# Three-bank exponentials in the last half of a four-layer transformer kernel, with the score ring and the probability buffers each made one tile

## The chip, the cores and the metric

One core of one Trainium2 chip. The metric is the device time of one launch in microseconds (us); lower is better. The kernel before takes 2383.65 us in the median of the four runs beside which the changed kernel was timed (2382.35 to 2387.67). Two names recur: PSUM is the memory into which the matmuls of TensorE (PE) write in this kernel, and a *bank* is a piece of it of 512 fp32 columns by 128 partitions, as the code cuts its tiles; SBUF holds the other tiles.

## The reference, cut to what matters

```python
def _A_ref(x, wqkv, w_phi, wo):      # linear attention on softmax features (cut)
    ...
def _B_ref(x, wqkv, wo):             # ordinary attention
    B, S, D = x.shape                # 1, 2048, 1024
    H = 32; Dh = D // H              # 32 heads of 32
    qkv = ...                        # (x @ wqkv) split by heads
    scores = jnp.einsum("bhqd,bhkd->bhqk", q, k) * (Dh ** -0.5)
    p = _softmax(scores, axis=-1)
    o = jnp.einsum("bhqk,bhkd->bhqd", p, v)
    return ... @ wo
def reference(...):                  # four layers: A, B, A, B
    x = A_x
    x = x + _A_ref(_layernorm(x), A_wqkv, A_w_phi, A_wo)
    x = x + _B_ref(_layernorm(x), B_wqkv, B_wo)
    x = x + _A_ref(_layernorm(x), A_wqkv, A_w_phi, A_wo)
    x = x + _B_ref(_layernorm(x), B_wqkv, B_wo)
```

Each B layer needs 32 x 2048 x 2048 exponentials, which is 1024 instructions of 128 x 1024 on ScalarE (ACT). That is the "first" and the "last" attention below; the rest is projections and the linear layers.

## The kernel before

The kernel is emitted by a scheduler in Python: it keeps a model of the engines' clocks, and at each point decides which matmul TensorE issues next. A *step* of attention takes two ring buffers, writes four row-tiled score matmuls (two into each), and starts two exponentials, one for each buffer. That holds for a unit of 512 queries; units of 256 or 128 queries fill the same buffers with more and shorter matmuls. The sums (probabilities times V, and times ones) go to two `work` banks. Whenever no step may start, TensorE does sums, then other projections, then fillers, which are matmuls without use, there for the clock that the trace shows (more of them took it from 0.84 to 1.00 in a stretch of one run below). Projections may borrow ring banks.

```python
e_t = [sb(f"E{i}", [P, 2, C]) for i in range(NE)]          # nine SBUF tiles, C = 512
e_s = Slots(clk, e_t)
...
ring_t = [pps.tile([P, 2, C], F32, tag=f"ring{i}", name=f"ring{i}") for i in range(3)]   # three PSUM tiles of two banks
work_t = [pps.tile([P, C], F32, tag=f"work{i}", name=f"work{i}") for i in range(2)]
...
def exp_chain(u, kks, e, buf):
    E = yield ("take", e_s)
    n = u.n * len(kks)
    yield ("op", "S", c_act(2 * n), lambda x: nc.scalar.activation(
        out=E[:, :, 0:n], in_=ring_t[buf][:, :, 0:n], func=ACT.Exp, scale=INV_SQRT_DH))
    ring.give(buf)
    sums.append((u, kks, e, E))

def emit_step():
    ...                                                    # cut: bookkeeping
    bufs = [ring.take(), ring.take()]
    for i, kk in enumerate(kks):
        c, m = divmod(kk, 2)
        for e in range(2):
            for j in range(2):
                r0 = 64 * (e ^ u.b) + 32 * j
                r = slice(r0, r0 + 32)
                nc.tensor.matmul(ring_t[bufs[e]][:, j, i * n:(i + 1) * n],
                    lhsT=K2[e][c][u.g // 4][r, u.g % 4, m, :], rhs=u.Q[r, e, 0:n],
                    start=True, stop=True, tile_position=(r0, 0), skip_group_check=True)
    for e in range(2):
        clk.start(exp_chain(u, kks, e, bufs[e]), st["t"] + PE_LAT)
```

The code writes no semaphores. The builder puts them in, from which tiles an instruction reads and writes: below, the same slices cut from one ring tile in place of three get other waits, and 2384 us become 3110.

The softmax here doesn't subtract the row's maximum and nothing guards it: scores larger than these inputs give would overflow.

Of the kernel before, what the change touches and what calls it, by code (L numbers as in the profile page):

```python
# [18 lines left out]
P = 128  # L19
D = 1024  # L20
# [197 lines left out]
class Task:  # L218
# [18 lines left out]
    (0, 4, (0,), False, False, (4, 5)), (0, 4, (0,), False, False, (0, 1, 3)), (0, 4, (0,), False, False, (2,)),  # L237
    (0, 4, (0,), False, False, (6, 7)), (4, 4, (0, 1), False, False, (0, 1, 2, 3)),
    (0, 4, (1,), True, False, (0, 1)), (0, 4, (1,), True, False, (2, 3)), (4, 4, (0, 1), False, False, (4, 5)),
    (0, 4, (1,), True, False, (4, 5)), (0, 4, (1,), True, False, (6, 7)), (4, 4, (0, 1), False, False, (6, 7)),  # L240
    (8, 4, (0, 1, 2), False, False, (0, 1, 2)), (8, 4, (0, 1, 2), False, False, (3, 4, 5)),
    (8, 4, (0, 1, 2), False, False, (6, 7)), (0, 4, (2, 3), True, True, (0, 1, 2, 3, 4, 5, 6, 7)),
    (4, 4, (3,), True, False, (0, 1)), (4, 4, (2,), True, True, (0, 1)),
    (4, 4, (2, 3), True, True, (2, 3, 4, 5, 6, 7)), (12, 2, (0, 1, 2, 3), False, True, (0, 1)),
    (8, 4, (3,), True, True, (4, 5, 6, 7)), (8, 4, (3,), True, True, (0, 1, 2, 3)),
    (14, 2, (0, 1, 2, 3), False, True, (2, 3, 4)), (14, 2, (0, 1, 2, 3), False, True, (0, 1)),
    (12, 2, (0, 1, 2, 3), False, True, (2, 3)), (12, 2, (0, 1, 2, 3), False, True, (4, 5)),
    (14, 2, (0, 1, 2, 3), False, True, (5, 6, 7)), (12, 1, (0, 1, 2, 3), False, True, (6, 7)),
# [3 lines left out]
    (0, 4, (0,), False, False, (4, 5)), (0, 4, (0,), False, False, (0, 1, 2, 3)),  # L252
    (0, 4, (0,), False, False, (6, 7)), (0, 4, (1,), True, False, (0, 1, 2, 3)),
    (4, 4, (0,), False, False, (0, 1)), (0, 4, (1,), True, False, (4, 5)),
    (4, 4, (0, 1), False, False, (2, 3, 4, 5, 6, 7)), (4, 4, (1,), True, False, (0, 1)),
    (8, 4, (0, 1, 2), False, False, (0, 1, 2, 3)), (0, 4, (2,), True, False, (0, 1)),
    (8, 4, (0, 1), False, False, (4, 5, 6, 7)), (0, 4, (2,), True, False, (4, 5)),
    (8, 4, (2,), True, False, (4, 5)), (0, 4, (1, 2), True, False, (6, 7)), (0, 4, (2,), True, False, (2, 3)),
    (0, 4, (3,), True, True, (2, 3, 6, 7)), (0, 4, (3,), True, True, (0, 1, 4, 5)),
    (8, 4, (3,), True, True, (4, 5)), (8, 4, (2, 3), True, True, (6, 7)), (4, 4, (2, 3), True, True, (2, 3)),  # L260
    (4, 4, (2, 3), True, True, (4, 6, 7)), (4, 4, (2,), True, False, (0,)), (4, 4, (2, 3), True, True, (1, 5)),
    (4, 4, (3,), True, True, (0,)), (8, 4, (3,), True, True, (0, 1, 2, 3)),
    (12, 4, (0, 1, 2, 3), False, True, (4, 5)), (14, 1, (0, 1, 2, 3), False, True, (2, 3, 6, 7)),
    (13, 1, (0, 1, 2, 3), False, True, (1, 2)), (15, 1, (0, 1, 2, 3), False, True, (0, 1, 2, 3, 6, 7)),
    (12, 1, (0, 1, 2, 3), False, True, (0, 1, 2)), (14, 1, (0, 1, 2, 3), False, True, (0, 1)),
    (12, 1, (0, 1, 2, 3), False, True, (3, 6, 7)), (13, 1, (0, 1, 2, 3), False, True, (0,)),
    (13, 1, (0, 1, 2, 3), False, True, (3, 6, 7)),
# [4 lines left out]
    ('AK', 0, 0, (0,), (0,)), ('AK', 0, 1, (0,), (0,)), ('fold', ('pk', 0)), ('fold', ('pk', 1)),  # L272
    ('AK', 0, 0, (0,), (1,)), ('AK', 0, 2, (0,), (0,)), ('AK', 0, 0, (1,), (0,)), ('AK', 0, 0, (1,), (1,)),
    ('AK', 0, 3, (1,), (1,)), ('AK', 0, 1, (1,), (1,)), ('fold', ('pq', 0)), ('fold', ('pq', 1)), ('DN', 0, 0),
    ('AK', 0, 1, (1,), (0,)), ('AK', 0, 2, (0,), (1,)), ('AK', 0, 2, (1,), (0,)), ('PQ', 0, 0),
    ('AK', 0, 3, (0,), (1,)), ('AK', 0, 1, (0,), (1,)), ('AK', 0, 2, (1,), (1,)), ('AK', 0, 3, (0,), (0,)),
    ('BP', 1, 0, (0,)), ('PQ', 0, 1), ('BP', 1, 0, (1,)), ('AK', 0, 3, (1,), (0,)), ('AO', 0, 0), ('DN', 0, 1),
    ('AO', 0, 2), ('BP', 1, 0, (2,)), ('AO', 0, 1), ('BP', 1, 0, (3,)), ('DN', 0, 2), ('BP', 1, 1, (0, 1)),
    ('BP', 1, 1, (2,)), ('BP', 1, 1, (3,)), ('PQ', 0, 2), ('BO', 1, 0, 1), ('PQ', 0, 3), ('BP', 1, 2, (0,)),
    ('BP', 1, 2, (1, 3)), ('BP', 1, 2, (2,)), ('DN', 0, 3), ('BO', 1, 10, 12), ('BO', 1, 1, 5), ('AO', 0, 3),  # L280
    ('BO', 1, 6, 7), ('BP', 1, 3, (0, 1, 2)), ('AK', 2, 0, (0,), (0,)), ('BO', 1, 7, 10),
    ('AK', 2, 0, (1,), (1,)), ('AK', 2, 0, (0,), (1,)), ('AK', 2, 0, (1,), (0,)), ('BP', 1, 3, (3,)),
    ('PS', 2, 0), ('AK', 2, 2, (0, 1), (0,)), ('PS', 2, 1), ('BO', 1, 5, 6), ('AK', 2, 2, (1,), (1,)),
    ('AK', 2, 1, (0, 1), (1,)), ('PS', 2, 2), ('AK', 2, 1, (0, 1), (0,)), ('BO', 1, 15, 16),
    ('AK', 2, 3, (1,), (0,)), ('DN', 2, 0), ('AK', 2, 3, (0,), (1,)), ('AO', 2, 0), ('AK', 2, 2, (0,), (1,)),
    ('AK', 2, 3, (0,), (0,)), ('BO', 1, 12, 15), ('PS', 2, 3), ('AK', 2, 3, (1,), (1,)), ('AO', 2, 3),
    ('DN', 2, 1), ('BP', 3, 0, (1,)), ('BP', 3, 0, (0,)), ('AO', 2, 2), ('BP', 3, 0, (2, 3)), ('AO', 2, 1),
    ('BP', 3, 1, (0, 1)), ('BP', 3, 1, (2,)), ('BP', 3, 1, (3,)), ('BP', 3, 2, (0, 1)), ('BO', 3, 0, 1),
    ('BO', 3, 4, 5), ('BP', 3, 2, (2, 3)), ('BO', 3, 8, 9), ('DN', 2, 2), ('BO', 3, 5, 7), ('BO', 3, 7, 8),
    ('DN', 2, 3), ('BO', 3, 9, 10), ('BP', 3, 3, (0, 1, 2, 3)), ('BO', 3, 15, 16), ('BO', 3, 2, 3),  # L290
    ('BO', 3, 12, 15), ('BO', 3, 3, 4), ('BO', 3, 10, 12), ('BO', 3, 1, 2),
# [3 lines left out]
class Unit:  # L295
    def __init__(self, l, vi, qt, w, ks, p, part, last):
        self.l, self.vi, self.qt, self.w, self.ks, self.p = l, vi, qt, w, ks, p
        self.q = qt // 4
        self.n = w * P
        self.g, self.b = divmod(p, 2)  # L300
        self.part, self.last = part, last
        kk = [2 * c + m for c in ks for m in range(2)]
        per = 4 // w
        self.steps = [tuple(kk[i:i + per]) for i in range(0, len(kk), per)]
        self.nsum = 0
        self.acc = None
        self.dst = None
        self.nburst = 0
        self.left = 0
        n = len(self.steps)  # L310
        m = -(-n // BURST)
        self.bursts = [2 * ((i + 1) * n // m - i * n // m) for i in range(m)]
        self.Q = None
        self.fast = False


@with_exitstack
def kernel(
# [60 lines left out]
    e_t = [sb(f"E{i}", [P, 2, C]) for i in range(NE)]  # L379
    phibd = e_t[0][:].rearrange("p a (g n) -> p (a g) n", n=P)  # L380
    e_s = Slots(clk, e_t)
# [14 lines left out]
    ring_t = [pps.tile([P, 2, C], F32, tag=f"ring{i}", name=f"ring{i}") for i in range(3)]  # L396
# [175 lines left out]
    def x_chain(l, t, key):  # L572
        yield ("key", key)
        xb = yield from grab(t_x)
# [30 lines left out]
    lo = [0]  # L605

    def slab_next(s):
        lst = slab_use.get(s, [])
        while lst and done_flag[lst[0]]:
            lst.pop(0)  # L610
        return lst[0] if lst else 1 << 30

# [15 lines left out]
    def slab_plan():  # L628
        want = sorted((slab_next(s), s) for s in slab_use)
        for nxt, s in want[:12]:  # L630
            if nxt >= 1 << 30 or nxt > lo[0] + HORIZON:
                break
# [6 lines left out]
            for i, sl in enumerate(slots):  # L639
                if not sl.avail or sl.users or sl.loading:  # L640
                    continue
                if i >= 4 and min((x for x in sl.limits if x > lo[0]), default=1 << 30) <= nxt:
                    continue
                if i in res and res[i] in pinned:
                    continue
                n2 = slab_next(res[i]) if i in res else (1 << 30) + (1 if i < 4 else 2)
# [561 lines left out]
    for l in (1, 3):  # L1208
# [4 lines left out]
        units[-1].fast = units[-2].fast = True  # L1213
    first_unit = {l: min(i for i, u in enumerate(units) if u.l == l) for l in (1, 3)}
# [199 lines left out]
    st = {"log": [], "t": 0.0, "mode": None, "last": -100.0, "ui": 0, "si": 0}  # L1414
# [18 lines left out]
    def step_ready():  # L1433
        if st["ui"] >= len(units):
            return False
        return st["si"] > 0 or unit_ready(units[st["ui"]])
# [9 lines left out]
    def exp_chain(u, kks, e, buf):  # L1446
# [3 lines left out]
            out=E[:, :, 0:n], in_=ring_t[buf][:, :, 0:n], func=ACT.Exp, scale=INV_SQRT_DH))  # L1450
        ring.give(buf)
        sums.append((u, kks, e, E))
# [57 lines left out]
    def emit_sum():  # L1510
# [6 lines left out]
        for i, kk in enumerate(kks):  # L1517
            c, m = divmod(kk, 2)
            end = u.left == 0 and i == len(kks) - 1
            for r0, ld in ((n0, None), (d0, ones)):  # L1520
                for j in range(2):
# [3 lines left out]
                        u.acc[r0 + 32 * j:r0 + 32 * j + 32, 0:n], lhsT=lh, rhs=E[:, j, i * n:(i + 1) * n],  # L1525
# [4 lines left out]
        clk.at(st["t"], lambda E=E: e_s.give(E))  # L1530
# [11 lines left out]
    def get_bank():  # L1542
# [8 lines left out]
        if not halves:  # L1551
# [4 lines left out]
            halves.extend([(b, 0), (b, 1)])  # L1556
# [3 lines left out]
        def rel():  # L1560
            split[b] -= 1
            halves.append((b, i))
            if split[b] == 0:
                halves.remove((b, 0))
                halves.remove((b, 1))
                ring.give(b)
        return ring_t[b][:, i, :], rel
# [38 lines left out]
    while True:  # L1606
# [3 lines left out]
        if ready and len(ring.free) >= 2:  # L1610
# [24 lines left out]
        if clk.heap:  # L1635
# [12 lines left out]
            continue  # L1648
        if left:
# [9 lines left out]
HORIZON = 200  # L1659
T_BULK = 8.0  # L1660
# [39 lines left out]
```

## Time and profile before

Most of the profile of before is in the prediction below; here is the frame for it. A *stretch* runs between the first and the last exponential of an attention.

| stretch of the kernel before | us | ScalarE busy | what sets its length |
|---|---|---|---|
| head (before the first exponential) | 289.4 | 131.5 | TensorE's projections |
| first attention | 1003.1 | 982.3 | ScalarE |
| middle | 126.6 | 58.8 | TensorE |
| last attention, first half | 482.9 | 478.3 | ScalarE |
| last attention, second half | 470.1 | 470.0 | ScalarE |
| tail | 8.3 | 0.0 | output |

Two terms recur. The *granted clock* is the share of full speed at which the trace shows TensorE's clock; a *low-clock window* is one of the stretches of 3.41 us that the trace records at half clock. In the list of waits, each line says who waited for whom, then the us in total, the number of waits and the longest:

```profile
PE ring L1469 <- ACT E L1449: 38.7, 103, 0.8
```

The ring's scores (line 1469) were held up by an exponential 103 times in 1024 steps. Nine times in ten the buffers were free when TensorE came to them.

### The profile page before, as it was taken

The numbers are of one execution on the slowest core, as the hardware profiler recorded it, in microseconds if no ns is written. First come the engines' busy times: TensorE is split into PE (matmuls) and PEld (weight loads), VectorE is DVE, ScalarE is ACT, GpSimd is POOL, SyncE is SP. The second block draws the span as 40 slices with busy tenths as digits, with TensorE's granted clock in tenths as the row PEclk, the third lists the DMA queues.
The fourth block names the chain that finished last, engine by engine and source line by source line (L and its number), as shares of the span: only waits on it lengthen the run. The fifth ranks groups of instructions, "written<-read, shape, count | busy, mean of one in ns | idle before, by whom it ended". The sixth has DMA issues, their size and how long they took to land.

```text
span 2380.4 us, 81956 instructions
## 1 busy us (share of the span) xinstructions
PE 2245.8 (94%) x35942; PEld 1009.7 (42%) x35985; DVE 1321.7 (56%) x2398; ACT 2121.0 (89%) x2501; POOL 400.5 (17%) x502
## 2 busy tenths in 40 slices
PE   6898999999999999998999899999999999999998
PEld 3544544334434333434555453433333333333555
DVE  6885554454545468696567855554533274363223
ACT  5543499999999999999998459999999999999998
POOL 3311101110211112122212210020200031120111
PEclk9999999899999999999999999999999999999999
DMA  6453364364454345354234655554465432230001
GB/s 249 145 157 108 132 193 171 112 199 130 147 141 145 108 133 155 115 142 80 91 101 130 173 135 166 192 140 137 123 198 174 135 125 81 64 110 33 19 22 31
DMA packets 216343, 306.05 MB, mean 129 GB/s; under 512 B 98736, under 2 KB 112560, under 8 KB 213296
## 3 DMA queue, kind: packets, MB, share of 16 engines
q1 hardware_dynamic: 191792, 200.14, 28.9%
q0 software_dynamic: 24192, 100.67, 12.6%
q8 instruction: 281, 4.60, 0.8%
q14 instruction: 78, 0.64, 0.1%
HBM read 195.36 MB, written 86.51 MB: 118 GB/s over the span
## 4 chain that ended last, share of the span: by engine, by line
PE 70%; ACT 16%; issue 7%; DVE 6%; DMA 1%; POOL 0%; SPq 0%; ACTq 0%; DVEq 0%; POOLq 0%
PE work L460 25%; PE work L1524 15%; ACT E L1449 14%; PE ring L1469 14%; PE work L463 7%; PE work L1642 3%; PE ring L463 3%; DVE blk L446 2%; ACT blk L772 1%; DVE sm L814 1%; PE work L1038 1%; DMA xnT<-blk 1%; DMA slab<-in_A_wqkv_dram 0%; DVE kvacc L446 0%; PE work L848 0%
## 5 line engine op out<-in xcount | busy, mean ns | idle before, releaser
L1449 ACT ACTIVATE E<-ring 128x1024 bf16<-128x1024 f32 x2048 | 1901.7, 1211 | 26.6 <-PE ring L1469 23.2
L1524 PE MATMUL work<-E,V 128*32 128x512 bf16 (+2 forms) x5888 | 551.1, 319 | 9.6 <-issue 3.7
L1524 PE MATMUL work<-E,ones 128*32 128x512 bf16 (+2 forms) x5888 | 551.0, 319 | 4.0 <-issue 4.0
L1469 PE MATMUL ring<-Q,K2b 32*128 32x512 bf16 (+2 forms) x2896 | 394.0, 315 | 49.4 <-ACT E L1449 38.1
L446 DVE TENSOR_TENSOR blk<-blk,work 128x512 f32<-128x512 f32 (+1 forms) x301 | 203.7, 680 | 375.5 <-PE work L1524 321.9
L1469 PE MATMUL ring<-Q,K2a 32*128 32x512 bf16 (+2 forms) x2896 | 407.8, 318 | 1.6 <-DMA Q<-qd 0.6
L1524 PEld LDWEIGHTS <-V 128*32 128x32 bf16 x5888 | 243.9, 97 | 158.0 <-issue 70.2
L446 POOL TENSOR_TENSOR blk<-blk,blk 64x512 bf16<-64x512 f32 (+2 forms) x180 | 175.1, 973 | 777.3 <-DVE blk L1314 689.4
L1278 DVE COPY blk<-work 128x512 f32<-128x512 f32 (+2 forms) x184 | 97.1, 528 | 346.4 <-PE work L1524 341.4
L1469 PEld LDWEIGHTS <-K2a 32*128 32x128 bf16 x2944 | 119.3, 91 | 385.1 <-issue 372.9
L1524 PEld LDWEIGHTS <-ones 128*32 128x32 bf16 x5888 | 239.5, 97 | 51.8 <-issue 5.9
L1314 DVE RECIPROCAL blk<-blk 128x128 f32<-128x128 f32 x254 | 229.4, 930 | 2.6
L1642 PE MATMUL work<-ident,ones 128*32 128x512 bf16 x3156 | 222.0, 382 | 2.8 <-DVE blk L446 0.9
L1469 PEld LDWEIGHTS <-K2b 32*128 32x128 bf16 x2944 | 163.3, 91 | 135.5 <-issue 128.7
L460 PE MATMUL work<-slab,blk 128*32 128x512 bf16 x2752 | 179.9, 381 | 0.5 <-DVE blk L1278 0.2
L460 PE MATMUL work<-slab,xnT 128*32 128x512 bf16 (+1 forms) x2560 | 156.5, 367 | 0.9 <-DVE kvacc L446 0.3
L460 PE MATMUL work<-xnT,slab 128*32 128x512 bf16 x2120 | 140.5, 384 | 4.2 <-DMA xnT<-blk 2.5
L463 PEld LDWEIGHTS <-xnT 128*128 128x128 bf16 x818 | 79.1, 99 | 89.9 <-issue 17.2
L460 PEld LDWEIGHTS <-blk 128*32 128x32 bf16 x3404 | 78.4, 96 | 90.5 <-issue 32.9
L463 PE MATMUL work<-slab,xnT 128*128 128x512 bf16 (+1 forms) x485 | 106.7, 373 | 5.5 <-DMA slab<-in_A_wqkv_dram 3.0
L1642 PEld LDWEIGHTS <-ones 128*32 128x32 bf16 x3156 | 71.2, 95 | 89.8 <-issue 40.7
L460 PEld LDWEIGHTS <-slab 128*32 128x32 bf16 x3016 | 70.8, 96 | 86.1 <-issue 35.8
(184 smaller groups left out, 2321.8 us busy)
## 6 DMA issues: line engine op xcount, KB each, us to landing
pd<-blk SPq DMA_DIRECT2D x154, 256.0 KB, 2.5
blk<-pd SPq DMA_DIRECT2D x154, 256.0 KB, 3.4
Q<-qd SPq DMA_DIRECT2D x121, 256.0 KB, 2.8
slab<-in_B_wqkv_dram POOLq DMA_DIRECT2D x30, 1024.0 KB, 6.6
qd<-blk SPq DMA_DIRECT2D x64, 256.0 KB, 2.8
x<-blk SPq DMA_DIRECT2D x48, 256.0 KB, 2.7
blk<-x SPq DMA_DIRECT2D x48, 256.0 KB, 3.8
blk<-in_A_x_dram SPq DMA_DIRECT2D x32, 256.0 KB, 3.9
```

Of the source, the lines that this page charges most:

```text
L446: return ("op", e, cost, lambda x: eng(x).tensor_tensor(out=o, in0=a, in1=b, op=op))
L460: nc.tensor.matmul(o[js], lhsT=l[:, js], rhs=r, start=st, stop=sp, tile_position=(0, 32 * j), skip_group_check=True)
L463: nc.tensor.matmul(o, lhsT=l, rhs=r, start=st, stop=sp, skip_group_check=True)
L772: yield ("op", "S", c_act(C), lambda x, s=s: nc.scalar.activation(out=e[:, s * C:(s + 1) * C], in_=src, func=ACT.Exp, scale=1.0 - 2.0 * s))
L814: yield ("op", "V", c_sb(1024), lambda x: nc.vector.reduce_sum(out=sm[:, 0:32], in_=e3, axis=AX.X))
L1038: nc.tensor.matmul(bank[:, o:o + P], lhsT=e[:, s * C + t * P:s * C + (t + 1) * P], rhs=kvm[:, (2 * gp + gi) * 2 + s, :], start=True, stop= ...
L1278: yield ("op", "V", c_ps(n), lambda e: nc.vector.tensor_copy(out=a, in_=bank[:, 0:n]))
L1314: yield ("op", "V", 0.06 + 0.0063 * P, lambda e, x=x: nc.vector.reciprocal(out=r[:, x:x + P], in_=r[:, x:x + P]))
L1449: yield ("op", "S", c_act(2 * n), lambda x: nc.scalar.activation(out=E[:, :, 0:n], in_=ring_t[buf][:, :, 0:n], func=ACT.Exp, scale=INV_SQR ...
L1469: nc.tensor.matmul(ring_t[bufs[e]][:, j, i * n:(i + 1) * n], lhsT=K2[e][c][u.g // 4][r, u.g % 4, m, :], rhs=u.Q[r, e, 0:n], start=True, st ...
L1524: nc.tensor.matmul(u.acc[r0 + 32 * j:r0 + 32 * j + 32, 0:n], lhsT=lh, rhs=E[:, j, i * n:(i + 1) * n], start=u.first, stop=end, tile_positi ...
L1642: nc.tensor.matmul(work[-1][32 * j:32 * (j + 1), :], lhsT=ones[:], rhs=idb, start=True, stop=True, tile_position=(0, 32 * j), skip_group_c ...
```

## The change

The intent: an exponential over three PSUM banks pays its fixed cost once, where exponentials over two banks pay it one and a half times for as many columns. (Alone, one of 1024 columns lasts 1.023 us in the traces and one of 1536 lasts 1.450; 512 columns are thus 0.427, and an estimate of the fixed part from these two is 1.023 - 2 x 0.427 = 0.17 us.) So from the middle of the last attention on, the six ring banks are used as two buffers of three instead of three buffers of two, and score tiles are streamed into them across the borders of steps. To allow both widths, the ring and the probability buffers E each become one tile, of which the buffers are slices. The rest of the diff is a new order of the work, a rule that an attention layer's input tiles wait for all output tiles of the layer before, and new rules for loading weight slabs.

```diff
-    e_t = [sb(f"E{i}", [P, 2, C]) for i in range(NE)]
+    E_all = sb("E", [P, 2 * NE, C])
+    e_t = [E_all[:, 2 * i:2 * i + 2, :] for i in range(NE)]
...
-    ring_t = [pps.tile([P, 2, C], F32, tag=f"ring{i}", name=f"ring{i}") for i in range(3)]
+    ring_all = pps.tile([P, 6, C], F32, tag="ring", name="ring")
+    ring_t = [ring_all[:, 2 * i:2 * i + 2, :] for i in range(3)]
...
+    def exp_wide(tiles, buf):
+        E = yield ("take", e_w)
+        k = len(tiles)
+        yield ("op", "S", c_act(C * k), lambda x: nc.scalar.activation(
+            out=E_all[:, 3 * E:3 * E + k, :], in_=ring_all[:, 3 * buf:3 * buf + k, :], func=ACT.Exp,
+            scale=INV_SQRT_DH))
+        ring.give(buf)
...
+    def emit_wide():
+        set_mode("row")
+        buf = ring.take()
+        tiles = []
+        while len(tiles) < 3 and step_ready():
...                                        # cut: next unit, next tile; tiles cross units
+            for i, kk in enumerate(kks):
+                nc.tensor.matmul(
+                    ring_all[:, 3 * buf + len(tiles), i * n:(i + 1) * n], ...)
+            tiles.append((u, kks, e, j))
...
+        clk.start(exp_wide(tiles, buf), st["t"] + PE_LAT)
...
-        if ready and len(ring.free) >= 2:
+        if ready and not wide[0] and st["ui"] >= WIDE_U:
+            if len(ring.free) == 3:
+                go_wide()
+        elif ready and wide[0]:
+            if ring.free:
+                emit_wide()
+                continue
+        elif ready and len(ring.free) >= 2:
             emit_step()
...                                        # cut: tables of the order, output-tile rule, slab rules
+WIDE = (3, 12)                             # from visit 12 of the last layer on
```

## The prediction

> **What bounds the kernel now.** I read the page first (busy shares, slices), then the stretches between the marks that the exponentials set, then the group of the exponentials, then the timeline where ScalarE had run dry. The page:
>
> ```profile
> PE 2245.8 (94%) x35942; PEld 1009.7 (42%) x35985; DVE 1321.7 (56%) x2398; ACT 2121.0 (89%) x2501; POOL 400.5 (17%) x502
> ...
> ACT  5543499999999999999998459999999999999998
> ```
>
> TensorE (PE) looks busier, but matmuls overlap in the records and 3156 of them are fillers (constants times ones, 222 us). ScalarE (ACT) is at nine tenths except in three places: before the first attention, between the two attentions, and at the end. The first and last exponential of each attention set the stretches (columns: length, then busy time and count of PE, PEld, DVE, ACT, POOL):
>
> ```profile
> 0.00:289.40 289.40, 249.87 (x1817) 141.66 (x1849) 199.84 (x387) 131.50 (x239) 72.36 (x106) 0.98 0.48 160
> 289.40:1292.50 1003.10, 961.03 (x16687) 418.41 (x16689) 591.26 (x1022) 982.27 (x1105) 169.61 (x199) 0.98 0.45 132
> 1292.50:1419.10 126.60, 117.12 (x863) 63.58 (x872) 90.43 (x196) 58.84 (x119) 27.68 (x41) 0.97 0.63 173
> 1419.10:1902.00 482.90, 466.95 (x6964) 183.17 (x6961) 224.99 (x436) 478.34 (x529) 42.15 (x59) 0.98 0.52 157
> 1902.00:2372.10 470.10, 446.76 (x9598) 201.23 (x9597) 212.22 (x352) 470.01 (x513) 88.74 (x98) 1.00 0.20 62
> 2372.10:2380.40 8.30, 4.09 (x31) 1.63 (x31) 2.90 (x5) 0.02 (x1) 0.00 (x0) 1.00 0.08 32
> ```
>
> So: head 289, first attention 1003 (ACT idle 21), middle 127, first half of the last attention 483 (idle 5), its second half 470 (idle 0.1), tail 8. Attention is ScalarE's; head and middle are TensorE's. In the last half 512 exponentials take 470.1 us: 0.918 us each. That rate lives from overlap in two ways:
>
> ```profile
> L1449 ACT ACTIVATE E<-ring 128x1024 bf16<-128x1024 f32 x2048 | 1901.7, 1211 | 26.6 <-PE ring L1469 23.2
> ```
> ```profile
> 344.64 1.94 ACT L1449 ACTIVATE E<-ring 128x1024 bf16<-128x1024 f32 x2 [2.48 <-PE ring L1469]
> 347.24 3.77 ACT L1449 ACTIVATE E<-ring 128x1024 bf16<-128x1024 f32 x4 [0.66 <-PE ring L1469]
> ```
> ```profile
> 344.15 0.39 PE L1469 MATMUL ring<-Q,K2a 32*128 32x512 bf16 x2
> 344.16 0.39 PE L1469 MATMUL ring<-Q,K2b 32*128 32x512 bf16 x2
> ...
> 346.75 0.39 PE L1469 MATMUL ring<-Q,K2a 32*128 32x512 bf16 x2
> 346.75 0.39 PE L1469 MATMUL ring<-Q,K2b 32*128 32x512 bf16 x2
> ```
>
> One exponential alone lasts 1.02 us (shortest of its group 1.018), two in a row 1.94; and all 2048 idled only 26.6 us before them, because the next scores stand ready in another ring buffer. Where they did not, the price shows: scores started at 344.15 and 346.75, the exponentials at 344.64 and 347.24, 0.49 us later. In the other direction a score matmul that waits for an exponential (103 times, 38.7 us in the list of waits) starts 51 to 52 ns after that exponential's end. The ring is three tiles of two banks; a step takes two of them, so its scores wait for the last but two and the last but one exponential, and the last one still runs meanwhile.
>
> [...] For 1024 columns [...] the trace has 1.023 and 0.918[...]. [...] the hardware lets TensorE write one ring bank while ScalarE reads another, as the trace of before does all along. [...] its low-clock records last 3.41 us or multiples, and column-tiled groups that start every 0.216 us start every 0.427 after them. Of the windows that lead into them nearly all had under half of their time streaming (counted from starts and columns at 2.4 per ns).
>
> **The change part by part.** I counted instructions in the built order of both kernels.
> 1. Wide exponentials. The last 512 exponentials of 1024 columns become 340 of 1536 and 2 of 1024. Back to back, 1536 columns would cost 0.918 + 512 x 0.833 ns = 1.345 us, so 342 x 1.345 = 460 us for 470: 10 us won. Scores go out in threes, not fours, so their array time grows from 55 to 73 us, and 165 more mode switches come; TensorE's fillers there fall from 113 to 87 us, so it has room.
> 2. Order. TensorE's work, counted in columns at 2.4 per ns, is 230 us in the head (as before) and 721 to 717 in the first attention without fillers; in the middle it falls from 112.0 to 96.9 us (15 won), while the first half of the last attention gets 15 more, with two stretches of 8 and 6 us between scores that will cost ScalarE some 11. ScalarE has 80 other operations in the first attention in both.
> If that were all: -10 - 15 + 11 + 2 (four more small exponentials), some 12 us faster.
> 3. Buffers. To allow both widths, the three ring tiles are made one tile of six banks, E one tile of 18. The semaphore counts in the built program show what that does. E is still tracked by region: an exponential waits for the one nine back, as before. The ring is not: every step's first score matmul now waits for the LAST exponential before it, though that one reads other banks. In before, a step waits for exponentials 600 and 601 while 602 runs; in after, the same step waits for 602. In the wide part, each set of three tiles waits for the exponential just before it, so two buffers act as one. This wait is in the program, and I take it as decisive.
>
> So scores and exponentials take turns. A narrow step: exponential's end to matmul 0.05, matmul to exponential 0.49, two exponentials 1.94: 2.48 us, for 1.83 now. TensorE's other work per step (mean 1.44 us in the first attention, only some dozen steps over 2.1) fits beside it. A wide step: 0.05 + 0.49 + 1.023 + 0.427 = 1.99 us for three tiles, for 1.38 now.
> - First attention: 512 x 2.48 = 1268. Ten of the 80 other ScalarE operations stand inside a pair, 5; the rest lie in the gaps. Transfers and other stalls, 12 of today's 21. Half clock: streaming share 0.59 on average, some 80 windows of 372 under a half; at a guessed 0.4 us each, 32. Sum 1317.
> - First half of the last attention: 256 x 2.48 = 634, the two stretches 8 (more of them lies beside the longer turns), half clock (36 windows) 12: 654.
> - Second half: 342 x 1.99 = 680. In steps of 128-query units (96 by my count) four matmuls of one tile now stand before those of the next, where they took turns: started in order, the last tile comes 3 x 0.053 x 2 = 0.32 us later, 31 us; with 256-query units 38. Half clock: streaming share 0.48, so perhaps every second window, 100 x 0.3 = 30. Sum 748; the two last guesses overlap, so I take 25 off: 723.
> - Head: 90 waits of ring matmuls for an eviction instead of 50, all for evictions of other banks; the 50 cost about 18 us of TensorE, so 15 more: 304. Middle: 127 - 15 + 8 for the same reason: 120. Tail 8.
> Sum 304 + 1317 + 120 + 654 + 723 + 8 = 3126 us of span, and run times lie 4 us over it: 3130.
>
> **Rivals.** (a) The wait is hidden: the PE arrives late at the scores anyway. For it: TensorE is 94% busy. Against: TensorE cannot be early enough any more, since no other work can replace scores that may not start; at least 0.54 us of idle ScalarE follows from every step, and 768 x 0.54 = 415 us. If I misread the wait, 2370. (b) The half clock spreads: with ScalarE slower TensorE streams less, falls under half in most windows, scores take 0.2 us longer and heavy steps no longer fit: 3250 to 3300. For it: shares of 0.48 to 0.59, near the edge; against: at half clock the same work counts double and the next window is full again. (c) TensorE becomes the bound in the wide part by 4/3 of the score time and the switches: some 330 us of work and switching in 700, no.
>
> **Range and chances.** The floor is 768 x 2.48 + 342 x 1.99 + 424 (head, middle, tail) = 3009 with nothing else; clock and stalls add 0 to 250. 3130, from 3000 to 3270. Faster by over 2% only if the built waits are not what runs: 0.02; within 2%: 0.02; slower: 0.96.
>
> **What would show it.** Right: exponentials as a group idle some 700 us before them, put down to the ring's scores, in pairs 0.54 us apart (timeline: pairs of 1.94, wide ones of 1.45 alone); score matmuls wait for E in nearly every step; ACT near 75% in attention; more low-clock windows; a middle near 120. Wrong: exponentials in long rows without gaps, or matmul to exponential well off 0.49 us.

Passages are cut from the prediction's third paragraph: statements that were not read from the traces or runs of this case, with what was drawn from them. No term of the sum is cut: it is 304 + 1317 + 120 + 654 + 723 + 8 = 3126 us of span, 3130 of run time. What the traces have for the numbers that remain:

- The 1.023 and 0.918 are us for an exponential of 1024 columns, alone and in a row. For the 0.833 ns per column, from which the 10 us won and the 0.427 come, the trace of before has ScalarE's casts of V, 371 ns for 256 columns and 585 for 512 in the mean, which is 0.836 ns a column; the changed kernel has exponentials of 1.023 us for 1024 columns and 1.450 for 1536 when alone, 0.834 ns a column. In a row, 1.345 was expected and 1.351 measured (split).
- One ring bank is written while another is read: in before 5678 of 5792 recorded score matmuls start while an exponential runs. In the changed kernel none of 5552 does.
- The 2.4 columns per ns: in before, matmuls of 512 columns (and groups of four column-tiled ones) mostly start every 0.216 us, 2.37 per ns; those of 128 columns, for which 0.053 is used, start at 100.21, 100.26, 100.32 and 100.37. After score matmuls the next column-tiled one starts 0.31 us later, and as much the other way, which is the cost of a mode switch here: 0.10 us more.
- The low-clock records are those of the trace of before. Of its full-clock windows of 3.41 us, 14 of 29 with under half of their time streaming were followed by half clock, and none of 646 with more. All 20 low-clock windows streamed for over half of their time (0.82 on average, with each matmul at twice its time), and after 14 of them the clock was full: that much stands behind "the next window is full again". The half as a limit is a reading of this one trace, and the us per window (32 for 80 windows, 12 for 36, 30 for 100) are guesses, which no trace gave.

## The result, and the profile after

The changed kernel takes 3192.18 us in the median of four runs (3179.52 to 3194.66), against 2383.65. The ratio is 1.338, with a 95% interval of 1.334 to 1.342. (Here and below a ratio is the mean time of one kernel's fast runs over that of the kernel before in the same rounds, so it is not quite the ratio of the medians that are quoted.) 3130 with a range of 3000 to 3270 was predicted.

The page of the changed kernel, busy shares and slices; PEclk is the granted clock of TensorE in tenths:

```profile
PE 2351.5 (74%) x35262; PEld 1078.3 (34%) x35302; DVE 1349.1 (42%) x2435; ACT 2213.8 (69%) x2313; POOL 407.4 (13%) x509
...
ACT  3442678887777777778874677777777666666665
...
PEclk7998999998999999999999998999998878978989
```

Where ScalarE stood at 9 throughout an attention it stands at 7, and at 6 in the wide half. TensorE's share fell as well, from 94 to 74%: neither engine is full any more, which is what two engines that take turns look like. The same by stretches (length, then busy time and count of PE, PEld, DVE, ACT and POOL, then granted clock, DMA share and GB/s):

```profile
0.00:346.10 346.10, 272.32 (x1789) 151.87 (x1820) 201.00 (x389) 126.09 (x232) 77.61 (x114) 0.89 0.48 138
346.10:1661.30 1315.20, 969.04 (x16672) 444.10 (x16672) 592.72 (x1021) 1034.61 (x1104) 173.51 (x205) 0.95 0.33 101
1661.30:1783.60 122.30, 102.81 (x824) 58.64 (x829) 89.51 (x190) 48.94 (x97) 27.77 (x41) 0.97 0.56 154
1783.60:2446.70 663.10, 474.15 (x7429) 205.79 (x7427) 241.81 (x476) 509.24 (x539) 48.71 (x63) 0.97 0.38 115
2446.70:3182.50 735.80, 529.09 (x8534) 216.23 (x8527) 221.18 (x356) 494.93 (x342) 79.80 (x87) 0.84 0.16 51
3182.50:3190.80 8.30, 4.09 (x31) 1.65 (x31) 2.90 (x5) 0.00 (x0) 0.00 (x0) 1.00 0.09 34
```

Of the 810 us lost, 312 are in the first attention, 180 and 266 in the two halves of the last, and 57 in the head. The middle gained 4. In the wide half ScalarE has 495 us of work in 736 us. The groups of instructions (busy us and mean ns, then the idle time before them and what ended most of it):

```profile
L1503 ACT ACTIVATE E<-ring 128x1024 bf16<-128x1024 f32 x1536 | 1491.8, 1021 | 429.7 <-PE ring L1610 414.8
L1610 PE MATMUL ring<-Q,K2a 32*128 32x512 bf16 (+2 forms) x1784 | 298.0, 353 | 499.4 <-ACT E L1503 498.5
L1541 ACT ACTIVATE E<-ring 128x1536 bf16<-128x1536 f32 x342 | 495.0, 1448 | 241.6 <-PE ring L1575 233.8
```

The exponentials idled 429.7 + 241.6 = 671 us before them, nearly all of it (414.8 + 233.8) for scores; before it was 26.6 us. The scores in turn idled for exponentials. Each waits for the other in a ring of two. In the list of waits, the scores' share is now

```profile
PE ring L1610 <- ACT E L1503: 519.9, 698, 1.8
PE ring L1575 <- ACT E L1541: 205.5, 278, 1.7
```

that is 698 of 768 narrow steps and 278 of 342 wide sets, where it was 103 of 1024. The timeline of one stretch of the first attention (start, length, then engine, line and number):

```profile
701.23 0.39 PE L1610 MATMUL ring<-Q,K2a 32*128 32x512 bf16 x2 [0.20 <-ACT E L1503]
...
701.73 1.94 ACT L1503 ACTIVATE E<-ring 128x1024 bf16<-128x1024 f32 x2 [0.56 <-PE ring L1610]
...
703.72 0.39 PE L1610 MATMUL ring<-Q,K2a 32*128 32x512 bf16 x2 [0.89 <-ACT E L1503]
...
704.23 1.94 ACT L1503 ACTIVATE E<-ring 128x1024 bf16<-128x1024 f32 x2 [0.56 <-PE ring L1610]
```

Follow one turn: two exponentials from 701.73 to 703.67; the next scores at 703.72, 0.05 later; their exponentials at 704.23, 0.51 later. A turn is 2.50 us, and 0.56 of it ScalarE stands still. The wide part, ScalarE alone, shows the same with one exponential a turn:

```profile
3001.56 1.45 ACT L1541 ACTIVATE E<-ring 128x1536 bf16<-128x1536 f32 x1 [0.59 <-PE ring L1575]
3003.61 1.45 ACT L1541 ACTIVATE E<-ring 128x1536 bf16<-128x1536 f32 x1 [0.59 <-PE ring L1575]
```

### The profile page after: what moved, and what is told of

The parts are those of the page before. It is cut to its first block, busy times and chain, and to the rows that moved or that the text cites. A ratio compares the mean times of both kernels' runs of the same rounds, so it can differ in the third digit from the quotient of the medians.

```text
span 3190.8 us, 79720 instructions
## 1 busy us (share of the span) xinstructions
PE 2351.5 (74%) x35262; PEld 1078.3 (34%) x35302; DVE 1349.1 (42%) x2435; ACT 2213.8 (69%) x2313; POOL 407.4 (13%) x509
## 4 chain that ended last, share of the span: by engine, by line
ACT 56%; PE 34%; issue 6%; DVE 2%; DMA 1%; ACTq 1%; POOL 0%; another core or an unknown queue 0%; DVEq 0%; POOLq 0%
ACT E L1503 42%; ACT E L1541 13%; PE ring L1610 10%; PE work L473 6%; PE ring L1575 6%; PE work L1665 4%; PE ring L473 3%; PE work L470 2%; PE work L1791 1%; DMA xnT<-blk 1%; ACT blk L823 1%; DVE blk L456 1%; ACTq L1503 0%; DMA slab<-in_A_wqkv_dram 0%; DVE kvacc L456 0%
## 5 line engine op out<-in xcount | busy, mean ns | idle before, releaser
L1503 ACT ACTIVATE E<-ring 128x1024 bf16<-128x1024 f32 x1536 | 1491.8, 1021 | 429.7 <-PE ring L1610 414.8
L1610 PE MATMUL ring<-Q,K2a 32*128 32x512 bf16 (+2 forms) x1784 | 298.0, 353 | 499.4 <-ACT E L1503 498.5
L1541 ACT ACTIVATE E<-ring 128x1536 bf16<-128x1536 f32 x342 | 495.0, 1448 | 241.6 <-PE ring L1575 233.8
L456 DVE TENSOR_TENSOR blk<-blk,work 128x512 f32<-128x512 f32 (+2 forms) x332 | 225.7, 681 | 770.4 <-PE work L1665 647.9
L1610 PEld LDWEIGHTS <-K2a 32*128 32x128 bf16 x1856 | 139.4, 91 | 807.3 <-issue 799.4
L1610 PE MATMUL ring<-Q,K2b 32*128 32x512 bf16 (+2 forms) x1784 | 296.3, 358 | 0.0
L1665 PEld LDWEIGHTS <-ones 128*32 128x32 bf16 x5696 | 244.1, 101 | 37.0 <-issue 1.3
L1575 PE MATMUL ring<-Q,K2a 32*128 32x128 bf16 (+2 forms) x992 | 160.7, 309 | 106.0 <-ACT E L1541 105.6
L1575 PE MATMUL ring<-Q,K2b 32*128 32x128 bf16 (+2 forms) x992 | 152.4, 308 | 100.5 <-ACT E L1541 99.9
L1575 PEld LDWEIGHTS <-K2a 32*128 32x128 bf16 x992 | 59.8, 97 | 178.2 <-issue 176.5
L1575 PEld LDWEIGHTS <-K2b 32*128 32x128 bf16 x992 | 56.2, 96 | 181.7 <-issue 179.4
```

Source lines behind the costliest of these rows:

```text
L456: return ("op", e, cost, lambda x: eng(x).tensor_tensor(out=o, in0=a, in1=b, op=op))
L1541: yield ("op", "S", c_act(C * k), lambda x: nc.scalar.activation(out=E_all[:, 3 * E:3 * E + k, :], in_=ring_all[:, 3 * buf:3 * buf + k, :] ...
L1575: nc.tensor.matmul(ring_all[:, 3 * buf + len(tiles), i * n:(i + 1) * n], lhsT=K2[e][c][u.g // 4][r, u.g % 4, m, :], rhs=u.Q[r, e, 0:n], st ...
L1610: nc.tensor.matmul(ring_t[bufs[e]][:, j, i * n:(i + 1) * n], lhsT=K2[e][c][u.g // 4][r, u.g % 4, m, :], rhs=u.Q[r, e, 0:n], start=True, st ...
L1665: nc.tensor.matmul(u.acc[r0 + 32 * j:r0 + 32 * j + 32, 0:n], lhsT=lh, rhs=E[j][0][:, i * n:(i + 1) * n], start=u.first, stop=end, tile_pos ...
```

## The experiments

**The theory (1):** the ring as one PSUM tile is nearly the whole loss. In the built program its matmuls wait for the latest reader of any part of the tile, also in other banks, so three buffers (or two wide ones) act as one. **Rivals:** the new order or its rules cost the time; the wide exponentials do; E as one tile does; in the head it is the order. All ten kernels that were run gave correct outputs. First the stretches of all that bear on the cause, in us, from the traces of the profiled runs (an attention is cut where three quarters of all score columns are done):

| kernel | head | first att. | middle | last, 1st half | last, 2nd half | median time |
|---|---|---|---|---|---|---|
| before | 289.4 | 1003.1 | 126.6 | 482.9 | 470.1 | 2383.65 |
| changed | 346.1 | 1315.2 | 122.3 | 663.1 | 735.8 | 3192.18 |
| before, one ring tile | 342.3 | 1316.5 | 136.2 | 653.0 | 650.7 | 3110.04 |
| before, one E tile | 293.7 | 998.7 | 127.1 | 483.0 | 470.9 | 2381.17 |
| changed, ring split | 290.9 | 991.5 | 111.2 | 496.5 | 461.9 | 2359.67 |
| changed, ring split, no wide | 285.7 | 991.0 | 110.7 | 495.2 | 471.1 | 2365.39 |
| changed, no wide | 339.1 | 1314.7 | 122.7 | 666.5 | 648.3 | 3100.97 |
| changed, ring split but for the head | 339.8 | 990.7 | 110.8 | 495.3 | 461.8 | 2409.63 |
| changed, more fillers | 340.2 | 1314.0 | 123.1 | 667.9 | 702.8 | 3152.96 |

### Undo one part: the ring split again (split)

```diff
-    ring_all = pps.tile([P, 6, C], F32, tag="ring", name="ring")
-    ring_t = [ring_all[:, 2 * i:2 * i + 2, :] for i in range(3)]
+    rps = ExitStack()
+    rp = rps.enter_context(tc.tile_pool(name="rpA", bufs=1, space=bass.MemoryType.PSUM))
+    ring_t = [rp.tile([P, 2, C], F32, tag=f"ring{i}", name=f"ring{i}") for i in range(3)]
...                                       # at the change to wide:
+        rps.close()
+        rp = rps.enter_context(tc.tile_pool(name="rpB", bufs=1, space=bass.MemoryType.PSUM))
+        ring_t[:] = [rp.tile([P, 3, C], F32, tag=f"wring{i}", name=f"wring{i}") for i in range(2)]
...
-            out=E_all[:, 3 * E:3 * E + k, :], in_=ring_all[:, 3 * buf:3 * buf + k, :], func=ACT.Exp,
+            out=E_all[:, 3 * E:3 * E + k, :], in_=ring_t[buf][:, 0:k, :], func=ACT.Exp,
```

(The score matmuls and the lent banks are named in the same way.)

> The changed kernel, same emission order, but the ring is three PSUM tiles of two banks until the wide part and two tiles of three banks in it; E stays one tile. In the built program a narrow step's scores wait again for the last but two and last but one exponential, a wide set for the last but one. Theory 1 (the one ring tile is the whole loss): 2370 us (2345 to 2390), that is 0.985 to 1.00 of before; head 289, first attention 1003, middle 112, first half of the last attention 495, second half 460; exponentials as a group idle under 50 us. Rival (the new order or the wide exponentials themselves are what costs): it stays above 3000 us, or, if only the wide part is to blame, at about 2640 with a second half above 700.

Measured: 2359.67 us (2355.44 to 2362.09; before 2381.06 in the same rounds), ratio 0.991 with an interval of 0.990 to 0.993. The whole loss is gone, and the kernel is a little faster than before. Its groups:

```profile
L1504 ACT ACTIVATE E<-ring 128x1024 bf16<-128x1024 f32 x1536 | 1430.6, 1191 | 18.8 <-PE ring L1614 17.2
...
L1545 ACT ACTIVATE E<-wring 128x1536 bf16<-128x1536 f32 x342 | 460.6, 1702 | 1.8 <-PE wring L1579 1.0
```

The idle time of the exponentials is 18.8 + 1.8 us instead of 671. Their records are longer (1702 ns a wide one, 1448 when taking turns) because neighbours overlap (342 of 1702 ns are 582 us, in 460.6 us of busy time); the rate is better: 342 in 461.9 us is 1.351 us each, 0.10 less than the 1.450 of one alone. So the order, the wide exponentials and E as one tile do not slow the kernel without the one ring tile, and the rivals fall as its cause. What the wide exponentials add while the ring is one tile is measured below (onering_narrow).

### One part alone: before, with one ring tile (before_onering)

```diff
-    ring_t = [pps.tile([P, 2, C], F32, tag=f"ring{i}", name=f"ring{i}") for i in range(3)]
+    ring_all = pps.tile([P, 6, C], F32, tag="ring", name="ring")
+    ring_t = [ring_all[:, 2 * i:2 * i + 2, :] for i in range(3)]
```

> The kernel before with one edit: the three ring tiles made one tile of six banks; order, E and everything else unchanged. Theory 1: 3110 us: head 346 (if waits for evictions of other banks are the head's loss as well), first attention 1315, middle 137, the two halves of the last attention 655 each, step period 2.49. Rival for the head (its extra 57 us come from the new order): head stays near 290 here. Rival for all (order or E): the time stays at 2384.

Measured: 3110.04 us, ratio 1.306 (1.303 to 1.310). The expected number was met to the microsecond, though not in each stretch (head 342, halves 653 and 651). These stretches of it answer to the head, the first attention and the last half of before:

```profile
0.00:342.34 342.34, 269.18 (x1817) 150.09 (x1846) 202.23 (x387) 133.41 (x240) 72.51 (x106) 0.91 0.41 135
342.34:1658.80 1316.46, 957.60 (x16683) 441.66 (x16687) 594.55 (x1022) 1035.29 (x1105) 169.10 (x199) 0.97 0.34 101
...
2448.03:3098.71 650.68, 432.83 (x9596) 206.61 (x9589) 211.51 (x352) 496.51 (x512) 86.51 (x97) 0.96 0.14 44
```

With the same work and order as in before (1817 matmul records in the head in both), the head is 53 us longer and the first attention 313. The head's loss belongs to the ring too, and not to the new order.

### One part alone: before, with one E tile (before_oneE)

```diff
-    e_t = [sb(f"E{i}", [P, 2, C]) for i in range(NE)]
+    E_all = sb("E", [P, 2 * NE, C])
+    e_t = [E_all[:, 2 * i:2 * i + 2, :] for i in range(NE)]
```

> The kernel before with one edit: the nine E tiles made one tile of 18 parts; ring and order as before. Theory 1 (in the built program E is tracked by region, so an exponential still waits for the sums nine exponentials back): same as before within 0.3%, 2381 us. Rival (a whole-tile wait for E as well): an exponential would wait for the sums of the one before it, 3500 us or more.

Measured: 2381.17 us, ratio 0.999 (0.997 to 1.001): the same. The same edit is free on the SBUF tile and costs 30% on the PSUM tile. Why the builder tracks the one by region and the other as a whole is not something these runs show; that it does is read from the semaphore counts in the built program, and the times agree.

### The order alone, and the wide part alone (split_narrow, onering_narrow)

Both have one edit, in the split and in the changed kernel:

```diff
-WIDE = (3, 12)
+WIDE = (9, 9)
```

> As the split kernel, but no wide exponentials: the new order alone, three ring tiles of two banks throughout. Theory 1: 10 us slower than the split kernel (second half of the last attention 470 instead of 460), so 2380. If the wide exponentials gain nothing because the four-for-three score matmuls and mode switches make TensorE the bound there, the two are equal or this one is faster.

Measured: 2365.39 us, ratio 0.994 (0.992 to 0.995). The new order is thus worth 0.6%, and the wide exponentials the rest up to 0.9%. In the last half they save 471.1 - 461.9 = 9 us, as expected. The medians differ by 6 and the two profiled runs by only 2: in the split kernel's the head was 5 us longer (6 low-clock windows in place of 3). Why the medians do not show the whole 9 is not settled by one profiled run of each.

> The changed kernel without its wide exponentials, ring still one tile. Theory 1: the last half goes back to turns of two: 256 steps of 2.49 and some low clock, 650 to 660 instead of 736, so 3110 us in all, about 80 faster than the changed kernel, head and first attention unchanged (346, 1315). Rival (the wide part is better even taking turns): slower than 3192.

Measured: 3100.97 us, ratio 1.303 (1.299 to 1.306), 91 us faster than the changed kernel. As long as the ring is one tile, wide exponentials cost 735.8 - 648.3 = 87 us in the last half. A turn's hand-over (from the end of an exponential over the scores to the start of the next one) is paid once for 2048 columns in a narrow step and once for 1536 in a wide set, so there are 342 turns of 2.044 us (699 us) where 256 of 2.494 (638) do the same work: 61 us. The rest goes with the clock, and so does a part of the 61: there were 67 low-clock windows in place of 14. A cleaner division comes from the run with more fillers below: with only 2 low-clock windows its wide half took 702.8 us, still 54 more than the narrow one. So some 54 of the 87 us are hand-overs and some 33 half clock.

### The head alone with one ring tile (head_one)

```diff
+    ring_all = rp.tile([P, 6, C], F32, tag="ring", name="ring")
+    ring_t = [ring_all[:, 2 * i:2 * i + 2, :] for i in range(3)]
...                                       # before the first step, when all three buffers are free:
+                rps.close()
+                rp = rps.enter_context(tc.tile_pool(name="rpH", bufs=1, space=bass.MemoryType.PSUM))
+                ring_t[:] = [rp.tile([P, 2, C], F32, tag=f"ring{i}", name=f"ring{i}") for i in range(3)]
```

> The split kernel (2360 us), but the ring is one tile of six banks in the head alone; it is replaced by three tiles just before the first score matmul. Theory 1 (the head's loss comes from projections that wait for evictions of other banks of the one tile, and from the half clock that follows): head 340 to 346 instead of 291, all else as in the split kernel, so 2412. Rival (the head's loss needs the long attention, or work is only shifted and caught up later): under 2385.

Measured: 2409.63 us, ratio 1.011 (1.010 to 1.013), that is 50 us over the split kernel.

```profile
0.00:339.85 339.85, 265.42 (x1789) 147.63 (x1820) 200.90 (x389) 126.08 (x233) 77.63 (x114) 0.92 0.48 141
339.85:1330.57 990.72, 954.02 (x16672) 418.83 (x16668) 587.32 (x1021) 981.33 (x1104) 176.30 (x205) 0.99 0.44 134
```

The head loses 49 us and the first attention nothing, so nothing is caught up later. The trace says how the head loses. Matmuls into ring banks were held 27 times for 18.6 us in before (24 times for 13.6 us in the split kernel), 71 times for 49.5 us here and 73 times for 49.4 us in the changed kernel, about half of them by VectorE's and half by ScalarE's evictions of projection results (33 and 38 here). The low-clock windows rose from 4 (6 in the split kernel) to 15 and 22.

### More fillers in the wide part (after_filled)

```diff
     def emit_wide():
+        if work:
+            for _ in range(2):
+                for j in range(4):
+                    nc.tensor.matmul(work[-1][32 * j:32 * (j + 1), :], lhsT=ones[:], rhs=idb, start=True, stop=True,
+                                     tile_position=(0, 32 * j), skip_group_check=True)
         set_mode("row")
```

> The changed kernel with one edit: ahead of each wide set's scores, where TensorE waits for the exponential anyway, two more filler groups of four column-tiled matmuls (0.43 us at full clock; 272 of the 342 sets get them). Theory 1 (of the 736 us of the last half, 37 come from the half clock that 67 windows of 3.41 us run at): under 20 low-clock windows there, median turn 2.04 as before, last half 700 to 710, so 3160 us in all. Rival (the fillers are late for the scores, or the half clock is free since TensorE idles anyway): last half 735 or longer.

Measured: 3152.96 us (3147.85 to 3158.07), ratio 1.323 (1.319 to 1.326). The last half:

```profile
2445.19:3147.96 702.77, 559.60 (x10694) 257.93 (x10687) 221.03 (x356) 494.96 (x342) 79.84 (x86) 1.00 0.17 54
```

More work for TensorE made it 33 us faster. The granted clock went from 0.84 to 1.00, the low-clock windows from 67 to 2, and the time between starts of exponentials from a median of 2044 ns to 2011, where I had expected no change. So half clock cost about 33 us of the 736: at half clock the scores, which now stand on the path in every turn, took longer to reach ScalarE (0.72 us instead of 0.50 from the first score of a wide set to its exponential in the changed kernel).

### Looking for a better version (split_w39, split_w30, split_w10)

The split kernel with the wide part begun earlier; of the three edits

```diff
-WIDE = (3, 12)
+WIDE = (3, 9)        # split_w39
+WIDE = (3, 0)        # split_w30: the whole last attention
+WIDE = (1, 0)        # split_w10: both attentions
```

each kernel has one.

> The split kernel (2360 us) with wide exponentials from a quarter of the last attention earlier (three quarters of it wide). Theory 1 (wide pays only where TensorE has work to spare; the first half of the last attention already has its longest stretches of other work between scores): between 2355 and 2375, no clear gain over the split kernel. Rival (wide pays wherever ScalarE is the bound): about 5 us faster, 2355.

Measured: 2360.42 us, ratio 0.991 (0.989 to 0.992): equal to the split kernel.

> The split kernel with the whole last attention wide. Theory 1: slower than the split kernel, 2365 to 2400, the loss being in the first half of the last attention (over 500 us for 496). Rival: 10 us faster, 2350.

Measured: 2382.82 us, ratio 1.000 (0.998 to 1.001). Slower than the split kernel by 23 us; 17 of them are in the first half of the last attention (513.4 for 496.5).

> The split kernel with wide exponentials in both attentions from the start (two ring tiles of three banks). Theory 1 (TensorE has no room in the first attention: it is at 96 to 97% there, and wide steps cost 4/3 of the score time and more mode switches): no gain, 2365 to 2420 us. Rival (wide exponentials pay wherever ScalarE is the bound): some 20 us faster than the split kernel, 2335 to 2345.

Measured: 2495.85 us, ratio 1.047 (1.045 to 1.049): slower, and by more than I expected. Its stretches from the first exponential on (first attention, middle, last attention):

```profile
288.03:1336.31 1048.28, 980.28 (x15395) 406.20 (x15404) 594.08 (x1017) 976.27 (x801) 175.47 (x205) 0.97 0.41 128
1336.31:1493.96 157.65, 133.21 (x959) 72.87 (x960) 102.48 (x219) 56.56 (x110) 33.99 (x47) 0.90 0.59 160
1493.96:2485.33 991.37, 934.27 (x15524) 383.00 (x15529) 478.82 (x841) 942.67 (x727) 134.33 (x154) 0.99 0.38 119
```

All three are longer than in the split kernel (991.5, 111.2 and 958.4), while ScalarE is busy for only 976 of 1048 us. In these runs wide exponentials did not pay wherever ScalarE is the bound; they paid in the last half, where little other work is left. What part of this is the score matmuls' greater time, what the two instead of three buffers from which projections can borrow, and what the order, which was made for narrow steps, was not separated. The trace gives a hint: of the 72 us that ScalarE idled in the first attention, 40 were ahead of its copies of K and V, for TensorE's projections, and only 24 ahead of exponentials; TensorE in turn waited 19 us, in two waits, for a weight slab from memory, which it did not do there in the split kernel. The best versions found are the split kernel and its variant with a longer wide part, each 0.9% faster than before.

## Why the prediction was right, point by point

The central step, "The ring is not: every step's first score matmul now waits for the LAST exponential before it", holds. It was read from the semaphore counts of the built program and not from the diff, where the new tile looks like a renaming. The edit alone makes 2384 into 3110 us, and its removal makes 3192 into 2360. The sum came out 65 us of span too low, 3126 for 3190.8. By terms:

| term | predicted | measured | |
|---|---|---|---|
| narrow turn | 2.48 us | 2.494 (median) | right |
| wide turn | 1.99 us | 2.044 (median), 2.011 at full clock | nearly |
| head | 304 | 346 (339 to 340 in three other runs of it) | **mis-sized by 42** |
| first attention | 1317 | 1315 | sum right, parts not |
| middle | 120 | 122 | right |
| last attention, first half | 654 | 663 | 9 low |
| last attention, second half | 723 | 736 | 13 low |

1. **The turns.** The scores started 52 ns after the exponential's end (median) and the exponentials 0.50 us after the scores, as predicted from two places in the trace of before. The exponential of 1536 columns lasted 1.450 us when alone, exactly the sum 1.023 + 0.427.
2. **The head is the term that failed.** The step was "all for evictions of other banks; the 50 cost about 18 us of TensorE, so 15 more". It scaled by the number of waits in the program. But of the 50 in before only 27 held TensorE at all, for 18.6 us (0.69 us each); the others were over when it came. Of the 90 after the change, 73 held it, for 49.4 us (0.68 each): here a wait for the newest eviction was in four cases of five a real one. That is +31 us instead of +15. The rest I had not counted at all: with TensorE so interrupted, 22 windows instead of 4 ran at half clock. Counted from starts and columns, the work done in those windows is 23.5 us at full clock for 5.7 before; at half clock it takes as long again (groups of column-tiled matmuls of 512 columns start every 0.427 us for 0.216), so my estimate is +18. Waits and half clock make 49 of the 57; the remainder is not traced. The half clock varies from run to run: the same head took 339 to 340 us in three other runs (onering_narrow, head_one, after_filled), with 15 or 16 low-clock windows, so 6 or 7 of the 57 belong to this one run.
3. **First attention.** 512 turns of 2.494 are 1277, 9 more than predicted (512 x 2.48 is 1270 and 256 x 2.48 is 635, where the prediction has 1268 and 634), and the rest 38 us instead of 49. Low-clock windows were 36, not 80. Two errors cancelled here, which is luck. The 80 were the windows expected to have under half of their time streaming. There were nearly as many, 73 at full clock (by the same count on the grid of the 3.41 us windows), but only 27 of them were followed by half clock: the half, read from the trace of before, was too high a limit here. Window by window in the whole changed kernel, by the same count: of the full-clock windows, 67 of 84 with under 0.4 of their time streaming were followed by half clock, 11 of 119 with 0.4 to 0.5, and none of 585 with more. By stretches, with the work counted at full clock: 36 of 385 windows were low in the first attention, which streamed for 59% of the time, 67 of 216 in the second half of the last attention (48%), and 2 of 206 there in the run with more fillers (66%).
4. **Second half of the last attention.** "started in order, the last tile comes 3 x 0.053 x 2 = 0.32 us later" was wrong: from first score to exponential it took 542 ns in sets of 128-query units and 496 in those of 512-query ones (medians at full clock), 0.05 more. The timeline of the changed kernel shows why, at the set before the exponential of 3001.56:

```profile
3001.02 0.21 PE L1575 MATMUL ring<-Q,K2a 32*128 32x128 bf16 x1 [0.67 <-ACT E L1541]
3001.04 0.24 PE L1575 MATMUL ring<-Q,K2b 32*128 32x128 bf16 x2
3001.08 0.21 PE L1575 MATMUL ring<-Q,K2a 32*128 32x128 bf16 x1
3001.11 0.23 PE L1575 MATMUL ring<-Q,K2b 32*128 32x128 bf16 x2
```

   The program has four matmuls of one tile, then four of the next, then of the third; they start as one of each, every 0.06 us, so a tile does not wait for the four of the tile before it. Against this the half clock was worse than my net guess: 67 windows and about 33 us, as the run with more fillers shows, where I had put 30 and then taken 25 off for overlap of the two guesses.
5. **Order.** "If that were all ... some 12 us faster": the split kernel is 21 us faster (2359.67 for 2381.06). The middle gained 15.4 (15 predicted), the first half of the last attention lost 13.6 (11 predicted), the second half gained 8.2 (10 predicted). Not foreseen are 12 us in the first attention, where I expected no gain; I have not traced which rule gave them. Part may be the run: before with one E tile, in the old order, took 998.7 there, 4 less than before.
6. **Rivals.** (a), a hidden wait, needed TensorE to come late to the scores; it came early in 698 of 768 steps. (b), the spreading half clock, happened in part, in the head and the wide half, and stayed in the range. (c), TensorE as the bound in the wide part, did not happen there; that it is why wide exponentials in both attentions lost time is not shown.

The split kernel computes the same, in the same order, with correct outputs and without waits for other buffers' banks, so the waits that cost some 830 us (3192.18 - 2359.67) guarded nothing.

## What to carry to other kernels

Before buffers are merged into one tile and sliced, look at what the built program then waits for: a ring whose every slot waits for the newest reader of any slot is a ring of one, and costs a full round of hand-overs in every turn (here 0.56 us of a turn of 2.50). If two shapes of buffers must share the same PSUM, close the pool and open another with the other shape at a point where all are free, as the split kernel does (2359.67 us). When waits are counted, ask how many will really hold the engine, and whether TensorE's clock will be lower as well with the idle time that they make (in the head here: 73 waits for 27, and a granted clock of 0.89 for 0.98).
